# MLP input transposes as column-tiled unit-matrix products, one exponential quad more, and new order constants in a fused attention and MLP block

## Chip, core and metric

The kernel runs on one NeuronCore of a Trainium2 chip. Its metric is the device time of one execution in microseconds. Before the change it is 803.54 us, the median of three runs (803.52 to 803.60).

## What is computed

One transformer block with adaptive layer norm on 2048 tokens of width 640, with 32 heads of width 20, and an MLP of width 1536 without an activation (gate times up). Inputs and output are bf16.

```python
mod = (silu(c) @ w_mod).reshape(1, 6, 1, 640)      # sa, ca, ga, sb, cb, gb
h = layernorm(x) * (1 + ca) + sa
x = x + ga * attention(h, wqkv, wo)                # softmax(q k' / sqrt(20)) v, then wo
h = layernorm(x) * (1 + cb) + sb
x = x + gb * (((h @ w_gate) * (h @ w_up)) @ w_down)
```

## The kernel before

**Chunks, items, units.** The queries are cut into five chunks of 512, 512, 512, 256 and 256 tokens (`CHUNKS`). An item is one chunk with four of the 32 heads, so there are 40 items, 8 for each chunk: chunk 0 has items 0 to 7, chunk 4 items 32 to 39. The scores of an item are cut into units of 512 columns in one PSUM bank: 64 units for an item of a chunk of 512, 32 for one of 256. TensorE computes them (L1496) as row-tiled products with a contraction over 32 rows, one head in each of four row groups.

**Two ways to the exponential.** Most units go to ScalarE in groups of two: one instruction of 1024 columns each (L1534), 804 in all. The rest goes to VectorE in quads of four units. VectorE adds a constant and writes the score as a 16-bit integer (L1558, four times), makes two terms of it by masking (L1590 and L1598, 2048 columns each), and the first term is multiplied with the integer's own bits read as bf16, on VectorE (L1595, one instruction) or on GpSimd (L1650, four pieces). Both terms then take part in the product with V, so a quad costs twice the value products of the same units on ScalarE. `QUADS` holds the number of quads of each item, 110 in all.

**Products with V** (L2233) are column-tiled: four products with 32 output rows each run side by side and add into one PSUM bank. When an item is complete, VectorE and GpSimd normalise it (L1728 to L1742), and DMAs put it in place as input of the output projection.

**The suffix of a chunk.** When the eight items of a chunk are complete, `suffix(ci)` does the rest for its tokens: the output projection with residual, the second layer norm (`xn2`), its transposition into `h2T`, gate and up products, their product (`hprod`), and the down product with residual. Most of these products are column-tiled too and are built by `quarters` (L955). Those of the last chunk, the tail, are full-width products (L951). The suffix of a chunk runs between the scores of the next one. That of the last chunk has nothing beside it.

**The transposes.** In `suffix`, `h2_round` (L1968) makes one block of 128 features of `h2T` from up to four token tiles of `xn2`: each a full 128 x 128 TensorE transpose, with a bf16 result in PSUM that is read through `bankh(b)`. One instruction on VectorE, or on ScalarE in the tail, evacuates the block (L1975 and L1977) with scale and shift. Chunks 0 and 1 have 5 rounds of 4 transposes, chunk 2 has 10 rounds of 2 (its MLP begins in two halves of 256 tokens), chunks 3 and 4 have 5 rounds of 2.

**What sets the order.** The program's order is planned while it is built. A list scheduler (`Sched` and `pick_pe`) plays the five engines with a duration in ns for each task and writes down the order of instructions on each engine; on the chip, each engine then takes its instructions in just this order and waits on semaphores. A column-tiled product is planned as a list of four instructions in mode "P", a transpose as a single one in mode "X", scores in mode "S", and a change of mode counts about 100 ns. A transpose is planned at 57 ns (`C128`), the evacuation of n columns of `h2T` at n x .78 + 55 ns. `STAGE` overrides the planner's parameters for each item while that item's value products run: for example how late a quad's scores may be (`D_LATE`), how many value products are taken at once (`PVMIN`, `PVMAX`, `PVCAP`), how long PE is held for a score that is about to be ready (`HOLD`), and how late other work may make a score (`PVTOL`, `X_LATE`). Where PE would have too little to do, the planner inserts products of the unit matrix as filler (L2600).

Of the kernel before, what the change touches and what calls it, by code (L numbers as in the profile page):

```python
# [329 lines left out]
def emit_program(nc, sched, nsem_dma=56):  # L330
# [97 lines left out]
    with nc.Block() as block:  # L428
# [20 lines left out]
        def _(e):  # L449
# [23 lines left out]
EAGER = 7  # L473
# [75 lines left out]
    8: {"PVCAP": 15, "PVMAX": 5, "Z_LATE": 19.94, "FILL_Z": 3656.07, "FILL_MIN": 3946.65, "TPRIO": 0.57, "EAGER": 16, "PVMIN": 1, "XBACK": 0, "STEAL_GAP": 194.45, "XDPRIO": 2.05, "D_LATE": 22},  # L549
    9: {"X_LATE": -14.35, "PVCAP": 12, "XBACK": 0, "HOLD": 110, "PVMIN": 1, "D_LATE": 24, "D_RES": 23, "FILL_MIN": 4183.51, "XDPRIO": 1.15, "PVTOL": 224, "FILL_Z": 2258.51, "Z_LATE": -44.48},  # L550
    10: {"PVMAX": 9, "X_LATE": -167.91, "EAGER": 5, "D_LATE": 21, "PVCAP": 7, "XBACK": 0, "HOLD": 110, "FILL_Z": 3693.44, "Z_LATE": -95.95, "PVMIN": 1, "XDPRIO": 1.25, "PVTOL": 199, "D_RES": 17},
    11: {"DL": 0.443, "X_LATE": 54.31, "FILL_MIN": 4086.76, "PVTOL": 270, "PVMAX": 6, "PVCAP": 14, "D_LATE": 22, "Z_LATE": -74.79, "EAGER": 4},
    12: {"DL": 0.459, "D_LATE": 11, "STEAL_GAP": 248.0, "HOLD": 125, "FILL_Z": 3256.59, "PVMIN": 1, "D_RES": 29, "FILL_MIN": 4938.23, "PVMAX": 8},
    13: {"DL": 0.417, "D_RES": 4, "HOLD": 129, "PVMAX": 4, "TPRIO": 0.51, "PVMIN": 5, "STEAL_GAP": 145.61, "PVCAP": 13, "FILL_MIN": 5235.75, "FILL_Z": 2424.75, "PVTOL": 324, "Z_LATE": -67.84, "XDPRIO": 1.14},
    14: {"D_LATE": 14, "D_RES": 16, "FILL_MIN": 4279.59, "EAGER": 11, "X_LATE": -16.94, "PVTOL": 374, "FILL_Z": 3396.29, "HOLD": 95, "XDPRIO": 1.32, "PVMAX": 10, "TPRIO": 1.87, "PVCAP": 9, "XBACK": 1},
    15: {"X_LATE": -189.21, "EAGER": 15, "Z_LATE": -100, "D_RES": 5, "HOLD": 110, "PVMAX": 4, "PVMIN": 4, "PVTOL": 199, "STEAL_GAP": 191.33, "D_LATE": 14, "FILL_Z": 3394.6},
    16: {"D_RES": 64, "HOLD": 133, "PVCAP": 11, "PVMIN": 3, "PVTOL": 299, "EAGER": 7, "Z_LATE": 153.49, "FILL_Z": 2909.17, "D_LATE": 20, "X_LATE": 34.41, "PVMAX": 8, "XBACK": 1},
    17: {"D_LATE": 19, "PVMAX": 10, "PVMIN": 5, "FILL_MIN": 4052.05, "EAGER": 4, "PVCAP": 9, "XBACK": 4, "Z_LATE": 171.58, "TPRIO": 1.29, "HOLD": 80, "X_LATE": -94.24, "FILL_Z": 2893.25, "PVTOL": 199},
    18: {"FILL_MIN": 3727.81, "D_RES": 10, "X_LATE": 15.11, "FILL_Z": 2885.8, "HOLD": 80, "Z_LATE": -17.94, "PVTOL": 74, "XBACK": 1, "STEAL_GAP": 228.57, "EAGER": 7, "XDPRIO": 1.03, "TPRIO": 0.81},
    19: {"DL": 0.471, "D_LATE": 16, "FILL_MIN": 4973.79, "HOLD": 140, "TPRIO": 1.09, "PVCAP": 15, "X_LATE": 9.04, "PVMAX": 10, "FILL_Z": 3225.84, "STEAL_GAP": 168.9},  # L560
# [6 lines left out]
    26: {"DL": 0.411, "D_RES": 18, "X_LATE": -208.68, "PVMAX": 9, "PVCAP": 14, "STEAL_GAP": 200, "FILL_MIN": 4600.59, "PVMIN": 5, "EAGER": 10},
    27: {"DL": 0.473, "D_LATE": 6, "PVMAX": 10, "EAGER": 4, "D_RES": 72, "PVTOL": 249, "PVMIN": 1, "FILL_MIN": 4986.69, "HOLD": 80, "X_LATE": 41.47},
    28: {"PVCAP": 13, "X_LATE": 57.95, "D_RES": 23, "HOLD": 80, "FILL_Z": 3480.79, "XBACK": 3},
    29: {"PVCAP": 14, "PVMAX": 6, "D_RES": 46, "FILL_MIN": 3820.529, "PVTOL": 299, "X_LATE": 68.11, "Z_LATE": -100, "STEAL_GAP": 248.04, "FILL_Z": 3365.14, "EAGER": 11, "D_LATE": 12, "XBACK": 2},  # L570
# [12 lines left out]
STG_G0, STG_G, XC_G = 12, -10, -20
# [12 lines left out]
def build_kernel(nc, A_x, A_wqkv, A_wo, B_x, B_w_gate, B_w_up, B_w_down, c, w_mod, out):  # L596
# [1239 lines left out]
    def suffix(ci):  # L1836
# [128 lines left out]
        def h2_round(k, t_lo, t_hi):  # L1965
            mms = []
            for tl in range(t_lo, t_hi):
                f = lambda e, b, tl=tl, k=k: e.transpose(bankh(b)[:, tl * 128:(tl + 1) * 128],  # L1968
                                                         xn2[:, tl, k * 128:(k + 1) * 128], ident[:])
                mms.append((C128, f))  # L1970
            sl = slice(t_lo * 128, t_hi * 128)
            nn = (t_hi - t_lo) * 128

            def after(r, k=k):
                f = lambda e: e.tensor_scalar(h2T[:, k, sl], bankh(r.b["b"])[:, sl], mcol[:, 3, k:k + 1],  # L1975
                                              mcol[:, 2, k:k + 1], op0=ALU.mult, op1=ALU.add)
# [699 lines left out]
```

## Time and profile before

| | before |
|---|---|
| median of 3 runs | 803.54 us |
| profiled execution | 803.48 us |
| its span, first to last instruction | 801.7 us |
| granted TensorE clock | 1.000 |
| busy share: PE, VectorE, ScalarE, GpSimd | 98%, 88%, 95%, 44% |
| exponentials on ScalarE (L1534) | 804, from 15.9 us to 764.2 us (starts) |
| transposes for the MLP (L1968) | 80: 60 + 10 in chunks 0 to 3, 10 in the tail |
| their evacuations on VectorE (L1975) | 10 of 512 columns, 538 ns each; 17 of 256 columns |

Records of one engine overlap: the next instruction starts before the last one has written its result. The duration of a record is therefore longer than the step from one start to the next, and a busy share near 100% can hide small pauses. Where that matters, the text works with differences of start times. PE's matmul records are modelled at their ends.

### The profile page before, as it was taken

The page shows a single profiled execution, that of the slowest core. Times are in us where ns is not written, and L with a number is a line of the kernel's source. Part 1 is how long each engine was busy: PE and PEld are TensorE (multiplying, and loading weights), DVE is VectorE, ACT ScalarE, POOL GpSimd, SP SyncE. Part 2 cuts the span into 40 slices and gives each one's busy share as a digit, 9 for nine tenths or more (in the row PEclk, how much of TensorE's full clock was granted, in tenths as well). Part 3 has the DMA queues.
Part 4 walks back from the last instruction along what each step waited for, and adds up shares of the span by engine and source line. Part 5 has one row for each costly group of instructions (what it writes and reads, how often), then busy time and mean ns, then how long its engine had stood idle before and what let it go on. Part 6 is the DMA issues. An engine that isn't in the chain of part 4 may idle for free.

```text
span 801.7 us, 29815 instructions
## 1 busy us (share of the span) xinstructions
PE 787.4 (98%) x12817; PEld 306.7 (38%) x12817; DVE 704.7 (88%) x1301; ACT 760.3 (95%) x849; POOL 352.6 (44%) x359
## 2 busy tenths in 40 slices
PE   8999999999999999999999999999999999999998
PEld 4433333222233233233233322333344444445577
DVE  7979977999999899997998999998799897987863
ACT  7899999999999999999999999999999999999922
POOL 3303266564444452256546443443545554442610
DMA  9734211113320225100400121001203453003110
GB/s 311 212 87 108 69 46 34 51 35 116 99 69 26 51 68 171 27 6 24 104 6 22 44 64 37 7 23 47 64 5 70 97 130 73 13 23 95 41 38 17
DMA packets 108505, 52.72 MB, mean 66 GB/s; under 512 B 76051, under 2 KB 108375, under 8 KB 108375
## 3 DMA queue, kind: packets, MB, share of 16 engines
q1 hardware_dynamic: 107447, 49.67, 23.4%
q8 instruction: 102, 1.67, 0.9%
q10 hardware_dynamic: 928, 1.15, 0.4%
q14 instruction: 28, 0.23, 0.1%
HBM read 39.88 MB, written 8.41 MB: 60 GB/s over the span
## 4 chain that ended last, share of the span: by engine, by line
PE 50%; ACT 40%; issue 5%; DVE 3%; DMA 1%; ACTq 0%; DVEq 0%
ACT PP L1534 40%; PE ps_all L1496 16%; PE ps_all L955 14%; PE ps_all L2233 11%; PE ps_all L1215 3%; PE ps_all L951 3%; PE ps_all L1151 2%; DVE DB L1558 1%; DMA wm<-in_w_mod_dram 1%; PE ps_all L1112 1%; DVE DSS L1590 1%; PE ps_all L976 0%; DVE DSS L1598 0%; DVE DSS L1595 0%; PE ps_all L1968 0%
## 5 line engine op out<-in xcount | busy, mean ns | idle before, releaser
L1534 ACT ACTIVATE PP<-ps_all 128x1024 bf16<-128x1024 f32 x804 | 740.3, 1133 | 4.1 <-PE ps_all L1496 3.1
L1650 POOL TENSOR_TENSOR DSS<-DB,DSS 128x512 bf16<-128x512 bf16 x252 | 286.7, 1159 | 322.3 <-DVE DSS L1598 266.9
L1558 DVE TENSOR_SCALAR DB<-ps_all 128x512 int16<-128x512 f32 x440 | 293.4, 683 | 46.8 <-PE ps_all L1496 45.2
L1496 PE MATMUL ps_all<-QT,KT 32*128 32x512 bf16 (+1 forms) x2560 | 313.3, 340 | 7.3 <-ACT PP L1534 4.9
L1496 PEld LDWEIGHTS ps_all<-QT,KT 32*128 32x128 bf16 x2560 | 81.4, 91 | 257.9 <-ACT PP L1534 220.6
L2233 PE MATMUL ps_all<-PP,Vf 128*32 128x512 bf16 (+1 forms) x2016 | 158.0, 344 | 0.1
L955 PE MATMUL ps_all<-h2T,stg 128*32 128x512 bf16 (+2 forms) x1936 | 119.4, 327 | 1.0 <-DVE DB L1558 0.8
L2233 PE MATMUL ps_all<-DSS,Vf 128*32 128x512 bf16 (+2 forms) x1088 | 85.0, 341 | 0.0
L1590 DVE TENSOR_SCALAR DSS<-DB 128x2048 int16<-128x2048 int16 x110 | 76.1, 692 | 1.1 <-PE ps_all L2233 0.4
L1598 DVE TENSOR_SCALAR DSS<-DB 128x2048 int16<-128x2048 int16 x110 | 75.6, 687 | 0.0
L2233 PEld LDWEIGHTS ps_all<-PP,Vf 128*32 128x32 bf16 x2016 | 44.9, 94 | 78.9 <-issue 73.4
L955 PE MATMUL ps_all<-wd,hprod 128*32 128x320 bf16 (+1 forms) x1380 | 61.9, 279 | 0.0
L1595 DVE TENSOR_TENSOR DSS<-DB,DSS 128x2048 bf16<-128x2048 bf16 x47 | 59.8, 1272 | 0.1
L1734 POOL TENSOR_TENSOR OTn<-OT,invT 128x512 bf16<-128x512 f32 (+1 forms) x39 | 38.4, 984 | 40.8 <-DVE invT L1732 40.7
L955 PEld LDWEIGHTS ps_all<-h2T,stg 128*32 128x32 bf16 x1936 | 41.3, 95 | 36.0 <-issue 23.4
L955 PEld LDWEIGHTS ps_all<-wd,hprod 128*32 128x32 bf16 x1380 | 30.1, 96 | 21.1 <-issue 14.1
L2233 PEld LDWEIGHTS ps_all<-DSS,Vf 128*32 128x32 bf16 x1088 | 27.6, 95 | 18.3 <-issue 8.6
L955 PE MATMUL ps_all<-wV,hT 128*32 128x320 bf16 (+1 forms) x704 | 32.1, 289 | 0.0
L955 PE MATMUL ps_all<-wo,Ocp 128*32 128x320 bf16 (+1 forms) x648 | 30.0, 283 | 0.7 <-DVE xck L1929 0.3
L1215 PE MATMUL ps_all<-hT,wq 128*32 128x512 bf16 x375 | 30.7, 383 | 0.0
L1728 DVE STREAM_TRANSPOSE OT<-ps_all 128x512 f32<-128x512 f32 (+1 forms) x40 | 24.1, 602 | 2.7 <-PE ps_all L2233 2.6
L2091 DVE TENSOR_TENSOR hprod<-ps_all,gsb 128x512 bf16<-128x512 f32 x32 | 21.7, 679 | 4.3 <-PE ps_all L955 4.3
(134 smaller groups left out, 535.4 us busy)
## 6 DMA issues: line engine op xcount, KB each, us to landing
stg<-in_B_w_gate_dram SPq DMA_DIRECT2D x44, 160.0 KB
stg<-in_B_w_up_dram SPq DMA_DIRECT2D x44, 160.0 KB
QT<-q_rows SPq DMA_DIRECT2D x22, 128.0 KB
KT<-k_rows SPq DMA_DIRECT2D x84, 32.0 KB
wm<-in_w_mod_dram SPq DMA_DIRECT2D x3, 800.0 KB
x<-in_A_x_dram SPq DMA_DIRECT2D x7, 320.0 KB
wd<-in_B_w_down_dram SPq DMA_DIRECT2D x1, 1920.0 KB
out_dram<-xck SPq DMA_DIRECT2D x12, 160.0 KB
```

Of the source, the lines that this page charges most:

```text
L955: return lambda e, b: e.matmul(ps[32 * x:32 * x + 32, b, c0 + o:c0 + o + w], lhs()[:, 32 * x:32 * x + 32], rhs() if w == n else rhs()[:, o ...
L1215: f = [lambda e, b_, k=k, x=x: e.matmul(ps[x:x + min(32, w - x), b_, :], wx[:, k, r0 + x:r0 + min(x + 32, w)], hT[tc][:, k, :], tile_posit ...
L1496: ems.append(lambda e, i=i, kt=kt: e.matmul(dstf()[:, i * u.n:(i + 1) * u.n], KT[32 * u.s:32 * u.s + 32, u.j, kt * 128:(kt + 1) * 128], QT ...
L1534: return e.activation(PPs[g % 2][:, cellp["p"], 0:nu * 512], ps[:, b0:b0 + nu, :].rearrange("p b c -> p (b c)"), AFT.Exp, scale=ESCALE)
L1558: return e.tensor_scalar(DBl[st_["slot"]][:, x * 512:(x + 1) * 512], bank(cell["b"]), EBIAS, 0.0, op0=ALU.add, op1=ALU.max)
L1590: return e.tensor_scalar(DSl[st_["ss"][0]][:, :], DBl[st_["slot"]][:, :], 0x7F, 0x3F00, op0=ALU.bitwise_and, op1=ALU.bitwise_or)
L1595: return e.tensor_tensor(d, DBl[st_["slot"]][:, :].bitcast(BF16), d, ALU.mult)
L1598: return e.tensor_scalar(DSl[st_["ss"][1]][:, :], DBl[st_["slot"]][:, :], 0x7F80, 2, op0=ALU.bitwise_and, op1=ALU.bitwise_or)
L1650: return e.tensor_tensor(d, DBl[st_["slot"]][:, x * w:x * w + w].bitcast(BF16), d, ALU.mult)
L1728: t1 = Task("dve", n * 1.1 + 70, lambda e: e.transpose(OT[:, 0:n], ps[:, BPV, 0:n].rearrange("p (b q r) -> p b r q", q=32, r=2)), [], prio ...
L1734: f3 = lambda e: e.tensor_tensor(OTn[:, 0:n].rearrange("p (b c r) -> p b r c", c=32, r=2), OT[:, 0:n].rearrange("p (b r c) -> p b r c", c= ...
L2233: ems.append(lambda e, i=i, kt=kt, stt=stt, stp=stp: e.matmul(ps[32 * s:32 * s + mc, BPV, 0:u.n], Vf[:, (kt * H + 4 * u.j + s) * VW:(kt * ...
```

## The change

The change has three parts.

It makes the transposes of chunks 0 to 3 products with the unit matrix. `quarters(128, ...)` takes 32 columns of the `xn2` tile at a time as the stationary operand and the unit matrix as the moving one, in four column tiles, so that each transpose becomes four instructions in mode "P". The result is float in PSUM, and the evacuation reads it as float. The planner counts 65 ns (`H2Q_US`) instead of 57 for one. The evacuation's planned duration stays. The tail keeps its transposes.

It gives item 32, the first of chunk 4, two quads instead of one: 111 quads in all.

It replaces the rows of items 8 to 39 in `STAGE`. The rows of items 0 to 7 stay.

```diff
 QUADS = ...
-         (1, 2, 2, 1, 3, 0, 2, 2))
+         (2, 2, 2, 1, 3, 0, 2, 2))
 HALF = [0, 0, 4, 0, 0]
 RESID, RES_G = 1, -20
+H2Q, H2Q_US = 1, 65.0
 ...
 STAGE = {
 ...
-    13: {"DL": 0.417, "D_RES": 4, "HOLD": 129, "PVMAX": 4, "TPRIO": 0.51, "PVMIN": 5, "STEAL_GAP": 145.61, "PVCAP": 13, "FILL_MIN": 5235.75, "FILL_Z": 2424.75, "PVTOL": 324, "Z_LATE": -67.84, "XDPRIO": 1.14},
+    13: {"DL": 0.417, "D_RES": 4, "HOLD": 129, "PVMAX": 4, "TPRIO": 0.51, "PVMIN": 5, "STEAL_GAP": 145.61, "PVCAP": 13, "FILL_Z": 2424.75, "Z_LATE": -67.84, "XDPRIO": 1.14, "X_LATE": 6.51},
 ...
-    38: {"D_RES": 60, "PVMAX": 7, "PVTOL": 375, "D_LATE": 14, "EAGER": 5, "TPRIO": 0.3, "FILL_MIN": 3948.58, "XBACK": 3, "X_LATE": 4.46, "HOLD": 65},
+    38: {"D_RES": 63, "PVMAX": 4, "PVTOL": 375, "D_LATE": 14, "EAGER": 5, "TPRIO": 0.3, "FILL_MIN": 3948.58, "XBACK": 3, "HOLD": 65},
 ...
         def h2_round(k, t_lo, t_hi):
             mms = []
             for tl in range(t_lo, t_hi):
                 f = lambda e, b, tl=tl, k=k: e.transpose(bankh(b)[:, tl * 128:(tl + 1) * 128],
                                                          xn2[:, tl, k * 128:(k + 1) * 128], ident[:])
-                mms.append((C128, f))
+                if H2Q and not tail:
+                    f = quarters(128, lambda tl=tl, k=k: xn2[:, tl, k * 128:(k + 1) * 128], lambda: ident[:], True, True, tl * 128)
+                mms.append((H2Q_US if H2Q and not tail else C128, f))
             sl = slice(t_lo * 128, t_hi * 128)
             nn = (t_hi - t_lo) * 128
 
+            def h2b(b_):
+                return ps[:, b_, :] if H2Q and not tail else bankh(b_)
+
             def after(r, k=k):
-                f = lambda e: e.tensor_scalar(h2T[:, k, sl], bankh(r.b["b"])[:, sl], mcol[:, 3, k:k + 1],
+                f = lambda e: e.tensor_scalar(h2T[:, k, sl], h2b(r.b["b"])[:, sl], mcol[:, 3, k:k + 1],
                                               mcol[:, 2, k:k + 1], op0=ALU.mult, op1=ALU.add)
-                fa = lambda e: e.activation(h2T[:, k, sl], bankh(r.b["b"])[:, sl], AFT.Identity,
+                fa = lambda e: e.activation(h2T[:, k, sl], h2b(r.b["b"])[:, sl], AFT.Identity,
                                             bias=mcol[:, 2, k:k + 1], scale=mcol[:, 3, k:k + 1])
                 return [evac(nn, nn * .78 + 55, f, fa, [r.last, r_sb.evac[0], r_cb.evac[0]] + ...)]
```

More of the change, by code (lines that the diff above doesn't have):

```diff
@@ L567 @@
[L567 to L570, printed above, removed]
@@ new lines @@
+    10: {"PVMAX": 9, "X_LATE": -167.91, "EAGER": 5, "D_LATE": 21, "PVCAP": 11, "XBACK": 0, "HOLD": 110, "Z_LATE": -46.62, "PVMIN": 1, "XDPRIO": 1.25, "PVTOL": 199, "D_RES": 26, "FILL_Z": 3952.08, "TPRIO": 0.58, "FILL_MIN": 3141.24},
+    11: {"DL": 0.443, "X_LATE": -1.25, "FILL_MIN": 4196.55, "PVTOL": 270, "PVMAX": 6, "PVCAP": 14, "Z_LATE": -74.79, "EAGER": 1, "XBACK": 0, "FILL_Z": 2873.49},
+    12: {"DL": 0.459, "D_LATE": 11, "STEAL_GAP": 248.0, "HOLD": 125, "FILL_Z": 3256.59, "PVMIN": 1, "D_RES": 29, "FILL_MIN": 4598.1, "PVMAX": 9, "XDPRIO": 1.16, "XBACK": 3, "X_LATE": 38.58},
@@ new lines @@
+    16: {"D_RES": 55, "HOLD": 133, "PVCAP": 11, "PVMIN": 3, "PVTOL": 249, "Z_LATE": 153.49, "FILL_Z": 2909.17, "D_LATE": 20, "X_LATE": 34.41, "PVMAX": 8, "XBACK": 1, "STEAL_GAP": 218.51, "EAGER": 9},
+    17: {"D_LATE": 25, "PVMAX": 10, "PVMIN": 5, "FILL_MIN": 4191.37, "EAGER": 4, "PVCAP": 9, "XBACK": 4, "Z_LATE": 171.58, "TPRIO": 1.29, "HOLD": 80, "FILL_Z": 2893.25, "PVTOL": 224, "X_LATE": -5.25},
+    18: {"FILL_MIN": 3438.35, "D_RES": 10, "X_LATE": 15.11, "HOLD": 80, "Z_LATE": -17.94, "PVTOL": 124, "XBACK": 0, "STEAL_GAP": 228.57, "EAGER": 4, "XDPRIO": 1.03, "TPRIO": 0.81, "PVMIN": 1, "PVMAX": 10},
@@ new lines @@
+    19: {"DL": 0.471, "D_LATE": 16, "FILL_MIN": 4050.2, "HOLD": 140, "TPRIO": 1.09, "PVCAP": 15, "X_LATE": -24.6, "PVMAX": 10, "FILL_Z": 3225.84, "STEAL_GAP": 168.9, "EAGER": 5},
+    20: {"DL": 0.391, "D_LATE": 10, "PVCAP": 10, "FILL_Z": 4009.3, "HOLD": 65, "STEAL_GAP": 143.97, "X_LATE": 53.99, "PVTOL": 249, "EAGER": 5, "D_RES": 23, "PVMIN": 5},
+    21: {"D_RES": 10, "PVCAP": 20, "HOLD": 156, "PVMAX": 4, "PVMIN": 3, "FILL_MIN": 4085.58, "FILL_Z": 1888.49, "Z_LATE": 146.94, "EAGER": 9, "TPRIO": 0.3, "XDPRIO": 1.17, "PVTOL": 174, "X_LATE": 29.81, "STEAL_GAP": 187.71},
@@ new lines @@
+    22: {"PVMAX": 4, "FILL_MIN": 2795.19, "D_RES": 11, "EAGER": 6, "PVCAP": 8, "PVTOL": 224, "STEAL_GAP": 189.38, "FILL_Z": 4295.57, "HOLD": 215, "PVMIN": 5, "X_LATE": 162.88, "TPRIO": 0.77, "D_LATE": 10, "XBACK": 0},
+    23: {"PVTOL": 197, "PVMAX": 7, "D_RES": 26, "Z_LATE": -13.47, "STEAL_GAP": 116.18, "FILL_MIN": 4540.5, "EAGER": 11, "XDPRIO": 2.88, "TPRIO": 0.57, "XBACK": 0, "X_LATE": -12.6, "HOLD": 125},
+    24: {"DL": 0.464, "PVMAX": 11, "PVMIN": 4, "FILL_MIN": 3530.42, "EAGER": 7, "HOLD": 125, "XDPRIO": 0.3, "D_LATE": 14, "D_RES": 17, "PVTOL": 174, "Z_LATE": -64.18, "XBACK": 2, "X_LATE": 24.59, "FILL_Z": 2375.67},
@@ new lines @@
+    25: {"DL": 0.549, "STEAL_GAP": 200, "HOLD": 84, "X_LATE": -22.95, "D_RES": 19, "FILL_MIN": 3973.44, "PVCAP": 13, "D_LATE": 18, "PVMIN": 3, "Z_LATE": 116.92, "PVMAX": 6, "XBACK": 1, "EAGER": 9, "TPRIO": 0.68, "FILL_Z": 3555.45, "PVTOL": 274},
+    26: {"DL": 0.411, "D_RES": 12, "PVMAX": 9, "PVCAP": 14, "STEAL_GAP": 200, "FILL_MIN": 3869.09, "EAGER": 10, "XBACK": 2, "HOLD": 125, "X_LATE": -0.14},
+    27: {"DL": 0.473, "D_LATE": 6, "PVMAX": 8, "EAGER": 2, "D_RES": 80, "PVTOL": 249, "PVMIN": 1, "FILL_MIN": 5500, "HOLD": 80, "X_LATE": -6.15, "TPRIO": 0.3},
@@ new lines @@
+    28: {"PVCAP": 16, "D_RES": 23, "HOLD": 95, "FILL_Z": 2998.15, "XBACK": 0, "EAGER": 6},
+    29: {"PVCAP": 14, "PVMAX": 6, "D_RES": 46, "FILL_MIN": 3820.529, "PVTOL": 299, "X_LATE": 68.11, "Z_LATE": -100, "STEAL_GAP": 274.39, "FILL_Z": 3365.14, "D_LATE": 6, "XBACK": 2, "HOLD": 140, "EAGER": 8},
+    30: {"X_LATE": 126.74, "PVCAP": 19, "FILL_MIN": 3191.14, "D_LATE": 16, "EAGER": 6, "PVMAX": 7, "STEAL_GAP": 165.05, "PVTOL": 174, "XDPRIO": 2.13, "PVMIN": 1, "Z_LATE": -100, "HOLD": 110},
+    31: {"D_RES": 19, "FILL_MIN": 5203.54, "D_LATE": 13, "PVMIN": 1, "X_LATE": 13.6, "HOLD": 185, "PVTOL": 274, "PVCAP": 13, "EAGER": 10, "FILL_Z": 3497.58, "XDPRIO": 3.33, "STEAL_GAP": 99.46},
@@ new lines @@
+    35: {"PVMIN": 2, "PVMAX": 8, "FILL_MIN": 2704.26, "STEAL_GAP": 162.94, "X_LATE": -108.93, "HOLD": 61, "D_LATE": 8, "XBACK": 4, "XDPRIO": 0.37, "EAGER": 8, "TPRIO": 0.3, "D_RES": 20},
+    36: {"DL": 0.524, "PVMIN": 3, "D_RES": 10, "X_LATE": 8.69, "PVMAX": 8, "HOLD": 153, "PVCAP": 15, "STEAL_GAP": 333.93, "PVTOL": 149, "TPRIO": 0.92, "FILL_Z": 3611.42, "D_LATE": 18},
+    37: {"D_LATE": 12, "PVTOL": 104, "PVCAP": 13, "X_LATE": -65.91, "TPRIO": 0.3, "XDPRIO": 1.88, "HOLD": 35, "STEAL_GAP": 181.37, "PVMIN": 5, "FILL_MIN": 4037.77, "FILL_Z": 3731.25, "PVMAX": 6, "EAGER": 9, "D_RES": 26, "Z_LATE": 204.75},
@@ L581 @@
+    38: {"D_RES": 63, "PVMAX": 4, "PVTOL": 375, "D_LATE": 14, "EAGER": 5, "TPRIO": 0.3, "FILL_MIN": 3948.58, "XBACK": 3, "HOLD": 65},
+    39: {"D_LATE": 13, "PVTOL": 208, "X_LATE": -38.86, "PVCAP": 17, "PVMAX": 5, "EAGER": 8, "XBACK": 3, "TPRIO": 0.48, "HOLD": 0, "D_RES": 11},
 }
```

33 lines of the change are left out of this document (7 added, 26 removed).

## The prediction

> **What bounds the kernel now.** I read the page first (busy shares, groups), then the answer for the exponential's line, then the waits of two stretches, then the chain of its last 38 us. The exponential's line, L1534:
>
> ```profile
> L1534 ACT ACTIVATE PP<-ps_all x804: 1002/1130/1346, 15.9 to 764.2; 128x1024 bf16<-128x1024 f32 x161
>   PEld ps_all L1496: 220.6, 621
> ```
>
> 804 exponentials start between 15.9 and 764.2 us: 803 steps in 748.3 us. A record's 1130 ns overlaps the next one; read one by one, the starts lie 903 ns apart at the tenth percentile and at the median. 803 x 0.903 = 725.1 us, so ScalarE loses only 23.2 us to lateness: 11.7 in chunk 0 (206 groups), then 3.5, 2.7, 2.6 and 2.8 in chunks 1 to 4 (198, 196, 102, 102 groups). The span is 15.9 + 725.1 + 23.2 + 37.5 us after the last start = 801.7; the profiled execution took 803.48 (1.8 around the span), the median is 803.54, so differences carry over unchanged. The second line says that 621 times a score product (L1496) waited until an exponential freed its banks: ScalarE sets the pace. But not everywhere. Waits at 396-576 us, then at 670-764:
>
> ```profile
> PEld ps_all L1496 <- ACT PP L1534: 62.7, 187, 0.7
> ```
>
> ```profile
> PEld ps_all L1496 <- issue: 16.4, 74, 0.4
> PEld ps_all L1496 <- ACT PP L1534: 5.5, 19, 0.4
> ```
>
> In chunk 2 nearly each of 196 groups waits for ScalarE; in chunk 4 only 19 of 102 do, and 74 scores follow PE's earlier work directly. The chain behind the last exponential is PE without a break:
>
> ```profile
> 766.20 2.08 PE ps_all L955 x76
> 768.27 3.23 PE ps_all L951 x23
> ...
> 776.03 3.24 PE ps_all L955 x92
> 779.27 19.77 PE ps_all L951 x180
> ```
>
> PE's starts agree: from 620 us to the end I find no unexplained gap (over 0.42 ns a column, as 512 columns take 216, plus a change between kinds of products) except 0.56 us and 1.08 us of filler (L2600) between 720 and 740. So up to about 610 us ScalarE is the bound, after it PE, with ScalarE just behind.
>
> **The quad (item 32).** Four units leave ScalarE: two groups less, 2 x 0.903 = 1.81 us. On PE two score slots go: each 0.216 plus its two changes of product kind, 0.2 (512 columns to a score 323 ns instead of 216; score of 256 columns to the rest 202 instead of 109), 0.83 in all; the four scores ride in other score slots on free rows. The second term adds one round of value products, 0.216. PE gains 0.62. VectorE gets 4 x L1558, one L1590, one L1598 and the product on itself or on GpSimd:
>
> ```profile
> L1558 DVE TENSOR_SCALAR DB<-ps_all 128x512 int16<-128x512 f32 x440 | 293.4, 683 | 46.8 <-PE ps_all L1496 45.2
> L1650 POOL TENSOR_TENSOR DSS<-DB,DSS 128x512 bf16<-128x512 bf16 x252 | 286.7, 1159 | 322.3 <-DVE DSS L1598 266.9
> L1595 DVE TENSOR_TENSOR DSS<-DB,DSS 128x2048 bf16<-128x2048 bf16 x47 | 59.8, 1272 | 0.1
> ```
>
> Start to start these take 0.601, 0.60, 0.60, 1.13 (VectorE) or 4 x 1.117 (GpSimd): 3.6 to 4.7 us of VectorE. Item 32 and those behind it run here:
>
> ```profile
> 668.00:684.00 16.00, 16.00 (x318) 6.74 (x316) 11.42 (x21) 16.00 (x18) 7.28 (x8) 1.00 0.31 70
> 684.00:764.00 80.00, 79.86 (x1892) 41.27 (x1888) 67.30 (x132) 79.71 (x87) 36.22 (x38) 1.00 0.18 43
> ```
>
> VectorE (third pair) has 17.3 us idle of 96: it hides the quad; uncovered, up to 4.7 us would come back as late banks. The worth lies between 0.62 (PE the bound) and 1.81 (ScalarE). Chunk 4 is nearer to PE: 0.62 + 19/102 x 1.19 = 0.84. If no row were free, the two slots would stay and nothing be gained.
>
> **The transposes.** 70 of them (5 blocks x 4, 4, 4, 2 tiles; the last chunk keeps its 10) become 280 column-tiled products. Before, around chunk 0's:
>
> ```profile
> 258.81 0.34 PE L1968 MATMUL ps_all<-ident,xn 128*128 128x128 bf16 x3
> 259.08 0.39 PE L1496 MATMUL ps_all<-QT,KT 32*128 32x512 bf16 x3
> ...
> 261.21 0.40 PE L1968 MATMUL ps_all<-ident,xn 128*128 128x128 bf16 x4
> 261.54 0.40 PE L2600 MATMUL ps_all<-ident 128*32 128x512 bf16 x4
> ```
>
> Transposes follow each other after 56 ns; the first column-tiled product behind one after 149, so leaving costs 93, and entering from a 512-column value product takes 333 instead of about 222, some 110. The same 128 columns as four column tiles (halved L955 products) also follow at 56: the product itself is free. Entries from column-tiled work number 7 before 764 us, exits to it 8: 7 x 0.11 + 8 x 0.093 = 1.5 us of PE at most. The 14 exits that lead to scores (163 ns) gain nothing: tiled work pays the same (166). What lateness there is to win: the 28 exponentials beside these transposes lost 0.99 us, at the average rate of chunks 1 to 4 (19 ns) it would be 0.53. I take 0.46, between 0 and 1.5. The Trainium skill (TensorEngine Tiling (Array Packing), Tiling Modes, Key Properties) says that changing the tiling mode drains TensorE; the 149 against 56 ns agrees.
>
> **Their evacuations.** L1975 now reads float:
>
> ```profile
> L1975 DVE TENSOR_SCALAR h2T<-ps_all,mcol 128x512 bf16<-128x512 bf16 x10 | 5.1, 538 | 1.0 <-PE ps_all L1968 0.9
> L1227 DVE TENSOR_SCALAR KPA<-ps_all 128x512 bf16<-128x512 f32 x13 | 8.8, 679 | 0.7 <-PE ps_all L1215 0.7
> ```
>
> Start to start 452 against 601 ns at 512 columns, 319 against 331 at 256: 10 x 0.149 + 15 x 0.012 = 1.7 us of VectorE. The order's cost stays nn x .78 + 55 = 454 ns, so VectorE falls behind by up to 0.75 us in each of chunks 0 and 1. Next transposes wait for its banks, scores queue behind them on PE, ScalarE behind those. An example: at 734 us, where the order counts 255 ns and the chip takes 319, one exponential came 0.32 us late. One such stall in each of two chunks is 0.6; between 0 and 1.7 I take 0.3, since VectorE has idle time in both (5.1 of 60 us at 240-300).
>
> **The order of items 8 to 39.** The trace can't show it; its rows bound it. Items 8, 13, 26 and 37 lose 0.70, 1.03, 0.59 and 0.92 us where the median item loses about 0.27: 2.2 us that single late waits made (the largest, 0.6 us at 342, is PE waiting for L1558). All items at the median would be 2.8 us less than now; all of chunks 1 and 2 at chunk 4's rate (27.6 ns a group instead of 15.6) 4.7 us more. DMA issues on SP move with the order; the engines are 18% busy at 684-764, so I count them at nothing; a late weight block would hold one PE round. I take -0.9, under half of the four items' excess and the filler at 734.
>
> Sum: -0.84 - 0.46 + 0.3 - 0.9 = -1.9: 803.5 - 1.9 = **801.6**.
>
> **Rivals.** (1) Given back: quad at PE's 0.62, transposes 0.46, evacuations at 1.3, order no better: +0.2, or +0.8 with the transposes at nothing; with evacuations at 0.5, -0.6: 803.0 to 804.2. For it: 74 direct follow-ups in chunk 4. Chance 0.22. (2) The transposes don't do what they say, since the order sets them between scores (14 exits already are): quad 0.84, evacuations 0.3: 803.0. Chance 0.12. (3) Slower: the new order reaches scores late. In chunks 1 and 2, PE's room per group is small; at chunk 4's rate +4.7 - 0.84 - 0.46 + 0.3 = 807.2. It decides from 2.6 us more lateness, 6.7 ns per group over 394 groups (22.3 instead of 15.6). Against it: 187 of 196 groups there wait for ScalarE, so most lateness is absorbed. Chance 0.10. (4) The four quarters run in series, 3 x 56 ns more for each of 70: 11.8 us of PE, of which chunk 3's 1.7 are uncovered: 803.3 to 813.4 with the rest as forecast, say 808. Against it: groups of four start within 30 ns of each other. Chance 0.02. The Trainium skill (Perfetto Trace Analysis, Optimizing Tensor Performance, Transposes) speaks against the change here: a logical transpose should use the transpose, not a standard matmul. The equal 56 ns don't bear that out.
>
> **How the numbers follow.** About 0.2% (1.6 us) is what a measurement of this kernel can tell from no change. Forecast 0.54, faster; rivals 1 and 2 0.34, within; 3 and 4 0.12, slower. Low end: transposes at 1.5 and the order at -2.2: -0.84 - 1.5 + 0.3 - 2.2 = -4.2, 799.3; I give 799.4. The high end goes past rival 1 to 804.8 and leaves rivals 3 and 4 out.
>
> **What would show it.** 802 exponentials; no L1968 in 128*128 form before 764 us; L1975 at about 680 ns with float input; the first 213 us (items 0 to 7) unchanged; the last exponential start 1 to 3 us earlier. If that start is 2 us earlier while the stretch behind it grows over 37.5 us by about 1, PE is the bound as read. Chunk 1 and 2 lateness over 22 ns per group would make the forecast wrong; over 0.5 us beside chunk 0's evacuations makes their term too small.

## The result, and the profile after

The changed kernel takes **805.57 us**, the median of ten executions (805.0 to 806.51). The kernel before took 803.51 beside it (ten, 803.46 to 803.62). The ratio is 1.0027, with a 95% interval of 1.0018 to 1.0036: slower by about 2 us, where 1.9 us less had been forecast. The profiled execution took 806.49 us with a span of 804.7. It lies 0.9 above the median: TensorE's granted clock was at half for 3.4 us in it. That need not be the whole reason, since two of the ten, with a mean clock of 1.000, took 806.32 and 806.38.

The answer for the exponential's line after the change comes first (minimum, median and maximum ns, then first and last start; below it the idle time of ScalarE by what ended it, and who waited for ScalarE):

```profile
L1535 ACT ACTIVATE PP<-ps_all x802: 1003/1127/1346, 15.9 to 767.3; 128x1024 bf16<-128x1024 f32 x161
  PE ps_all L1497: 6.6, 12
  PEld ps_all L1497: 222.3, 613
```

There are 802 exponentials, two fewer, as forecast, yet the last one starts 3.1 us later (767.33 against 764.22). Read from the start times as before, with 0.903 us for each step, lateness (what the exponentials start later in all than at that even pace) is 28.1 us instead of 23.2. By chunks:

| lateness, us | all | chunk 0 | 1 | 2 | 3 | 4 | beside the MLP transposes |
|---|---|---|---|---|---|---|---|
| before | 23.2 | 11.72 | 3.48 | 2.67 | 2.56 | 2.79 | 1.05 |
| after | 28.1 | 11.73 | 5.57 | 4.09 | 3.61 | 3.12 | 4.91 |

The last column adds up five stretches, one for each set of rounds of `h2_round` and its evacuations (from the first transpose to 2 us behind the last evacuation): 0, 0.25, 0.18, 0.28 and 0.34 us before; 1.29, 1.18, 0.91, 0.31 and 1.21 after. So the bill of the two profiled executions is: -1.81 for the two exponentials, +3.86 beside the transposes, +1.05 elsewhere in items 8 to 39, -0.09 behind the last exponential; together +3.0, and 806.49 - 803.48 is 3.01. The first 213 us are unchanged. Some 1.4 us of the "elsewhere" are the stretch at half clock, read at the end of this document.

What happened beside the transposes is seen in the groups of after (busy us, mean ns of one, idle before):

```profile
L1981 DVE TENSOR_SCALAR h2T<-ps_all,mcol 128x512 bf16<-128x512 f32 x10 | 7.6, 803 | 0.7 <-PE ps_all L956 0.6
L956 PE MATMUL ps_all<-ident,xn 128*32 128x128 bf16 x240 | 7.2, 222 | 0.4 <-DVE h2T L1981 0.2
L1981 DVE TENSOR_SCALAR h2T<-ps_all,mcol 128x256 bf16<-128x256 f32 x10 | 4.8, 527 | 0.0
```

The 240 products are the 60 transposes of chunks 0 to 2, four each, and the fours start some 56 ns apart, as forecast. The evacuation of 512 columns has a mean of 803 ns, not about 680 as the prediction's marker had it, and 538 before. Start to start it takes 719 ns for 512 columns and 452 for 256, against 452 to 456 and 319 before, and against 454 and 255 in the plan. The longest of the waits that end with these evacuations (us in all, times, longest), after and then before; `h2Tt` is chunk 3's block:

```profile
PEld ps_all L956 <- DVE h2T L1981: 2.6, 7, 0.9
PE ps_all L1497 <- DVE h2T L1981: 1.5, 4, 0.6
PEld ps_all L956 <- DVE h2Tt L1981: 1.5, 3, 0.9
```

```profile
PEld ps_all L1968 <- DVE h2T L1975: 0.7, 3, 0.3
PEld ps_all L955 <- DVE h2T L1975: 0.6, 2, 0.3
```

With the smaller rows, TensorE's products and weight loads, which overlap, have 8.0 us of such waits where they had 2.4: TensorE waits for what VectorE has yet to evacuate, and five times the waiting product is a score (four of them above). One such place on the timeline of after, in chunk 1 (start, duration, engine, and in brackets the idle time before):

```profile
433.65 0.57 PE L956 MATMUL ps_all<-ident,xn 128*32 128x128 bf16 x28
433.94 2.97 DVE L1981 TENSOR_SCALAR h2T<-ps_all,mcol 128x512 bf16<-128x512 f32 x4 [0.62 <-PE ps_all L956]
...
435.62 0.39 PE L1497 MATMUL ps_all<-QT,KT 32*128 32x512 bf16 x3 [0.19 <-DVE h2T L1981]
...
436.97 0.40 PE L956 MATMUL ps_all<-h2T,stg 128*32 128x512 bf16 x4 [0.62 <-DVE h2T L1981]
...
437.30 0.39 PE L1497 MATMUL ps_all<-QT,KT 32*128 32x512 bf16 x3
...
437.73 1.02 ACT L1535 ACTIVATE PP<-ps_all 128x1024 bf16<-128x1024 f32 x1 [0.66 <-PE ps_all L1497]
```

Four evacuations run back to back on VectorE. TensorE reaches the gate and up products (436.97), which read `h2T`, and stands idle for 0.62 us. The score planned behind them (437.30) comes late, and the exponential that wants it starts after ScalarE has been idle for 0.66 us.

The other views shown before. TensorE's waits at 670 to 764 us:

```profile
PEld ps_all L1497 <- issue: 14.0, 64, 0.4
...
PEld ps_all L1497 <- ACT PP L1535: 7.8, 30, 0.4
```

and the chain behind the last exponential:

```profile
769.22 2.07 PE ps_all L956 x76
...
782.29 19.77 PE ps_all L952 x180
```

Before, 19 scores waited for ScalarE here and 74 followed TensorE's earlier work; now 30 and 64. The pieces of the chain have the same lengths (those between are 3.23 and 3.24 us for 23 and 92 products, as before), and the stretch behind the last exponential is 37.4 us as before (37.5).

### The profile page after: what moved, and what is told of

It is laid out like the page before. It is cut to its first block, busy times and chain, and to the rows that moved or that the text cites. A ratio compares the mean times of both kernels' runs of the same rounds, so it can differ in the third digit from the quotient of the medians.

```text
span 804.7 us, 30172 instructions
## 1 busy us (share of the span) xinstructions
PE 787.9 (98%) x12987; PEld 306.6 (38%) x12987; DVE 712.2 (89%) x1307; ACT 759.7 (94%) x847; POOL 356.5 (44%) x363
## 4 chain that ended last, share of the span: by engine, by line
PE 63%; ACT 29%; DVE 4%; issue 3%; POOL 0%; ACTq 0%; DVEq 0%; POOLq 0%
ACT PP L1535 29%; PE ps_all L1497 20%; PE ps_all L956 18%; PE ps_all L2239 14%; PE ps_all L1216 3%; PE ps_all L952 3%; PE ps_all L1152 2%; DVE h2T L1981 1%; PE ps_all L2604 1%; DVE DB L1559 1%; PE ps_all L1113 1%; PE ps_all L2606 0%; PE ps_all L977 0%; DVE DSS L1599 0%; DVE DSS L1591 0%
## 5 line engine op out<-in xcount | busy, mean ns | idle before, releaser
L1651 POOL TENSOR_TENSOR DSS<-DB,DSS 128x512 bf16<-128x512 bf16 x256 | 291.2, 1157 | 332.2 <-DVE DSS L1599 276.2
L956 PE MATMUL ps_all<-h2T,stg 128*32 128x256 bf16 (+2 forms) x1980 | 120.5, 325 | 0.9 <-DVE h2T L1981 0.6
L2239 PE MATMUL ps_all<-DSS,Vf 128*32 128x512 bf16 (+2 forms) x1104 | 87.1, 341 | 0.4 <-DVE DSS L1599 0.3
L1591 DVE TENSOR_SCALAR DSS<-DB 128x2048 int16<-128x2048 int16 x111 | 77.7, 700 | 2.0 <-PE ps_all L2239 1.4
L1599 DVE TENSOR_SCALAR DSS<-DB 128x2048 int16<-128x2048 int16 x111 | 77.5, 698 | 0.0
L1596 DVE TENSOR_TENSOR DSS<-DB,DSS 128x2048 bf16<-128x2048 bf16 x47 | 57.3, 1223 | 0.1
L956 PEld LDWEIGHTS ps_all<-h2T,stg 128*32 128x32 bf16 x1980 | 43.4, 96 | 35.6 <-issue 22.8
L1735 POOL TENSOR_TENSOR OTn<-OT,invT 128x512 bf16<-128x512 f32 (+1 forms) x39 | 36.6, 939 | 36.5 <-DVE invT L1733 36.2
```

The source lines that it names most:

```text
L956: return lambda e, b: e.matmul(ps[32 * x:32 * x + 32, b, c0 + o:c0 + o + w], lhs()[:, 32 * x:32 * x + 32], rhs() if w == n else rhs()[:, o ...
L1591: return e.tensor_scalar(DSl[st_["ss"][0]][:, :], DBl[st_["slot"]][:, :], 0x7F, 0x3F00, op0=ALU.bitwise_and, op1=ALU.bitwise_or)
L1596: return e.tensor_tensor(d, DBl[st_["slot"]][:, :].bitcast(BF16), d, ALU.mult)
L1599: return e.tensor_scalar(DSl[st_["ss"][1]][:, :], DBl[st_["slot"]][:, :], 0x7F80, 2, op0=ALU.bitwise_and, op1=ALU.bitwise_or)
L1651: return e.tensor_tensor(d, DBl[st_["slot"]][:, x * w:x * w + w].bitcast(BF16), d, ALU.mult)
L1735: f3 = lambda e: e.tensor_tensor(OTn[:, 0:n].rearrange("p (b c r) -> p b r c", c=32, r=2), OT[:, 0:n].rearrange("p (b r c) -> p b r c", c= ...
```

## The experiments

Each row of `STAGE` for items 8 to 39 is called an order constant here. "Planned" is what the list scheduler counts for a task, "run" is what the chip takes. Every median stands beside the kernel before on the same chip (803.49 to 803.53). The experiments that take the transposes back to bf16 come first.

**The new order with true transposes in the column tiles.** The plan and the order are those of after; only the operation and its result in PSUM differ.

```diff
-f = quarters(128, lambda tl=tl, k=k: xn2[:, tl, k * 128:(k + 1) * 128], lambda: ident[:], True, True, tl * 128)
+f = [lambda e, b, tl=tl, k=k, x=x: e.transpose(bankh(b)[32 * x:32 * x + 32, tl * 128:(tl + 1) * 128],
+         xn2[:, tl, k * 128 + 32 * x:k * 128 + 32 * x + 32], ident[:], tile_position=(0, 32 * x)) for x in range(4)]
...
-return ps[:, b_, :] if H2Q and not tail else bankh(b_)
+return bankh(b_)
```

> The changed kernel, with the 280 products replaced by 280 transposes in the same four column tiles, so that PSUM again holds bf16. Durations planned and order of instructions are those of the changed kernel. Theory A (VectorE's evacuation of float with column scalars steps 719 and 452 ns where the order counts 454 and 255, so VectorE falls behind, PE waits for its banks and ScalarE for PE): evacuations back to about 452 and 319 ns, lateness beside the transposes from 4.9 back to about 1.1 us, no half-clock stretch, time about 801.7. Theory B (four instructions per transpose cost PE): 805 as in the changed kernel. Theory C (the new order constants are the loss): 805.

Measured: 802.05 us (801.34 to 804.51, 11 executions), ratio 0.9985 [0.9976, 0.9994]. The evacuations take some 452 and 319 ns again, lateness falls from 28.1 to 23.2 (1.4 of it is the stretch at half clock, which this profile lacks), and beside the transposes from 4.91 to 1.27. The group of the evacuations:

```profile
L1983 DVE TENSOR_SCALAR h2T<-ps_all,mcol 128x512 bf16<-128x512 bf16 x10 | 5.0, 537 | 1.3 <-PE ps_all L1972 1.3
```

The order of instructions is that of after to the last one, so 3.5 us of the change's time hang on what the product leaves, float instead of bf16.

**The new constants and the quad without the products.** `H2Q` is 0, all else as after, planned anew.

```diff
-H2Q, H2Q_US = 1, 65.0
+H2Q, H2Q_US = 0, 65.0
```

> The changed kernel with full-width transposes as before; the 111th quad and the new constants stay. A and B: lateness beside the transposes about 1.1 us, the quad's 1.8 us kept, about 801.8. C: 805 or more.

Measured: 811.81 us (4 executions), 1.0103 [1.009, 1.0117]. One wait of ScalarE for value products, in item 26 at 604 to 613 us, makes 3.4 us of it; the rest is spread over many shorter ones (the next, at 698 us, is 1.6) and 1.45 us behind the last exponential. That one wait left out, lateness beside the transposes is 1.05, as before. The number would fit theory C, but the version with full transposes in the order of after, further below, speaks against it. This run doesn't say what the constants are worth, since the plan around them changed: a transpose planned as one task of 57 ns in its own mode gives another order than four column-tiled products of 65 ns in mode "P".

**The products alone, with the old constants and the old quads.**

```diff
-         (2, 2, 2, 1, 3, 0, 2, 2))
+         (1, 2, 2, 1, 3, 0, 2, 2))
...
-STAGE rows 8 to 39 of after
+STAGE rows 8 to 39 of before
```

> The kernel before with the column-tiled products alone: 110 quads and the old constants. A and B: lateness beside the transposes 4 to 5 us instead of 1.1, about 807. C: 803.5.

Measured: 816.83 us (815.27 to 819.12, 5 executions), 1.0172 [1.0158, 1.0186]: neither forecast came. ScalarE's waits at 604 to 622 us:

```profile
ACT PP L1535 <- PE ps_all L2239: 9.7, 1, 9.7
```

and what TensorE does meanwhile, from this run's timeline:

```profile
609.60 0.39 PE L1497 MATMUL ps_all<-QT,KT 32*128 32x256 bf16 x4
609.92 1.49 PE L956 MATMUL ps_all<-h2T,stg 128*32 128x256 bf16 x48
...
614.98 0.29 PE L956 MATMUL ps_all<-ident,xn 128*32 128x128 bf16 x8 [1.21 <-DVE h2T L1981]
...
616.66 0.95 PE L956 MATMUL ps_all<-h2T,stg 128*32 128x256 bf16 x28 [1.06 <-DVE h2T L1981]
...
618.42 0.84 PE L2239 MATMUL ps_all<-PP,Vf 128*32 128x256 bf16 x24
```

The order runs the suffix of chunk 2 for 8.5 us without a score in between; the value products that free ScalarE's output buffers come behind it. Waits for VectorE's evacuations are some 2.3 us of that, the rest is how it was planned. Here too the plan changed together with what was to be measured.

**The true duration of the evacuations in the plan.** All as after, the evacuation planned at 719 and 452 ns.

```diff
-return [evac(nn, nn * .78 + 55, f, fa, ...
+return [evac(nn, nn * 1.043 + 185 if H2Q and not tail else nn * .78 + 55, f, fa, ...
```

> The changed kernel with the evacuation planned at 719 ns for 512 columns and 452 for 256 (n x 1.043 + 185) instead of 454 and 255. A, if the wrong plan is what hurts: the planner puts other work around the longer evacuations, lateness beside the transposes 1 to 2.5 us, 802 to 803.5. A, if the longer evacuation itself hurts however it is planned: 804.5 to 805.5. B and C: 805.

Measured: 819.14 us (4 executions), 1.0194 [1.018, 1.0208]: a miss. Again ScalarE waits in item 26, once: the exponential behind the one at 610.8 us comes 10.3 us late. A plan that knows the truth is no better with constants that were chosen for a plan that doesn't.

These three cost 8 to 16 us, of which single waits make 3.4, 9.8 and 10.3, in orders that the change of a planned figure or of the constants had upset. The next four therefore leave the order of before or of after untouched and change only what an instruction does: the function that a planned task issues is replaced, its planned mode and duration stay.

**The new order with full transposes.** Where after issues four products, one full-width transpose with a bf16 result stands; planned as in after.

```diff
-f = quarters(128, lambda tl=tl, k=k: xn2[:, tl, k * 128:(k + 1) * 128], lambda: ident[:], True, True, tl * 128)
+f = [lambda e, b, tl=tl, k=k: e.transpose(bankh(b)[:, tl * 128:(tl + 1) * 128], xn2[:, tl, k * 128:(k + 1) * 128], ident[:])]
...
-return ps[:, b_, :] if H2Q and not tail else bankh(b_)
+return bankh(b_)
```

> The changed kernel's order of instructions with one full-width transpose in place of each four products (bf16 in PSUM again); 111 quads and the new constants. Theory A (the float evacuations are the loss, the form of the product on PE matters little): lateness beside the transposes about 1.2 to 1.8 us instead of 4.9; against e4_tiled_transpose only the two changes of tiling, about 0.1 us each where the order put a transpose beside column-tiled work, so 802 to 803. If changes of tiling cost as much as the forecast allowed (1.5 us): 803.5. If the half-clock stretches come from column-tiled unit products: none here; if from the order: some of the runs at 0.998 again.

Measured: 801.92 us (801.61 to 802.6, 11 executions), 0.998 [0.9971, 0.9989]. The exponential's line:

```profile
L1535 ACT ACTIVATE PP<-ps_all x802: 1002/1136/1345, 16.3 to 763.2; 128x1024 bf16<-128x1024 f32 x161
  PE ps_all L1497: 3.1, 5
```

ScalarE waits for scores 5 times (3.1 us) where after has 12 (6.6 us). The order and the quad without the products are thus 1.6 us faster than before, and the products take 3.65 us from that. This version is faster than both kernels; it and the one with tiled transposes differ by 0.13 us, which these executions don't tell apart.

Its start times say where the 1.6 us are: two exponentials fewer save 1.81, lateness is 23.6 instead of 23.2, and the stretch behind the last exponential is 0.1 shorter. The order itself won no lateness.

**The old order with the products.** The reverse: before, each transpose's task issues the four products, and the evacuation reads float.

```diff
+if not tail:
+    def f(e, b, tl=tl, k=k):
+        q = quarters(128, lambda: xn2[:, tl, k * 128:(k + 1) * 128], lambda: ident[:], True, True, tl * 128)
+        return [g(e, b) for g in q][-1]
...
-f = lambda e: e.tensor_scalar(h2T[:, k, sl], bankh(r.b["b"])[:, sl], ...
+f = lambda e: e.tensor_scalar(h2T[:, k, sl], (bankh(r.b["b"]) if tail else ps[:, r.b["b"], :])[:, sl], ...
```

> The order of instructions of the kernel before, kept exactly, with four products in place of each transpose and float evacuations. Theory A: lateness beside the transposes 4 to 5 us instead of 1.05, evacuations stepping 719 and 452 ns, 806.5 to 807.5, without the single 10 us wait of e2_products_only, which is the order's. If that wait came with the products themselves: 815 or more. Theory C (the new constants are the loss): 803.5.

Measured: 806.82 us (806.56 to 807.53, 5 executions), 1.0042 [1.003, 1.0055]. The group of its evacuations and the two largest sums of waits for them:

```profile
L1979 DVE TENSOR_SCALAR h2T<-ps_all,mcol 128x512 bf16<-128x512 f32 x10 | 7.5, 802 | 0.5 <-PE ps_all L955 0.5
```

```profile
PEld ps_all L955 <- DVE h2T L1979: 3.2, 7, 0.8
PE ps_all L955 <- DVE h2T L1979: 1.5, 4, 0.5
```

The products cost 3.3 us in the old order too, with the same 802 ns; lateness beside the transposes is about 4 us instead of 1.05.

**The old order with tiled transposes.** As the last, with the four column-tiled transposes and a bf16 result.

```diff
+if not tail:
+    def f(e, b, tl=tl, k=k):
+        return [e.transpose(bankh(b)[32 * x:32 * x + 32, tl * 128:(tl + 1) * 128],
+                            xn2[:, tl, k * 128 + 32 * x:k * 128 + 32 * x + 32], ident[:],
+                            tile_position=(0, 32 * x)) for x in range(4)][-1]
```

> The order of instructions of the kernel before, kept exactly, with four column-tiled transposes (bf16) in place of each full-width one. It measures the changes of tiling alone: 803.0 to 803.5 if ScalarE hides them, 802.0 if all of PE's 1.5 us counts. If four instructions cost PE (theory B): 804 or more.

Measured: 803.43 us (803.3 to 804.45, 11 executions), 1.0001 [0.9992, 1.001]. Column tiles in place of full transposes, with nothing else, make no difference that shows, though TensorE is rid of the changes of tiling: the step to column-tiled work behind a transpose is 56 ns instead of 149, and the one from a 512-column value product into a transpose 216 to 226 instead of 324 to 333. Lateness is 23.1 against 23.2: the saved changes are worth next to nothing on the time.

**After, with constants for scale and shift.** The evacuations still read float, but multiply by 1.0 and add 0.0 in place of the columns of `mcol` (chunks 0 to 3 then lack the second layer norm's modulation).

```diff
-f = lambda e: e.tensor_scalar(h2T[:, k, sl], h2b(r.b["b"])[:, sl], mcol[:, 3, k:k + 1], mcol[:, 2, k:k + 1], ...
+f = lambda e: e.tensor_scalar(h2T[:, k, sl], h2b(r.b["b"])[:, sl], mcol[:, 3, k:k + 1] if tail else 1.0,
+                              mcol[:, 2, k:k + 1] if tail else 0.0, ...
```

> The changed kernel with the float evacuation's scale and shift columns replaced by the constants 1 and 0 (it leaves out the second layer norm's scale and shift in chunks 0 to 3). If the two column scalars are what makes 719 ns of the forecast's 601: steps of about 601 and 331 ns, lateness beside the transposes 2 to 3 us, 803 to 804. If reading float is the whole price: 719 and 452 as in the changed kernel, 805.5.

Measured: 802.67 us (802.36 to 803.75, 11 executions), 0.9991 [0.9983, 1.0].

```profile
L1981 DVE TENSOR_SCALAR h2T<-ps_all 128x512 bf16<-128x512 f32 x10 | 6.4, 682 | 1.0 <-PE ps_all L956 1.0
```

Now the instruction reads no column, like the row that the prediction priced it by (L1227, which multiplies by one constant and takes 679 ns): 682 ns, and start to start 598 and 331. So the forecast's price was right for constants and wrong for columns.

**bf16 with constants, and float with one column.** The version with tiled transposes and the constants; and after with the scale's column kept and the shift a constant (chunks 0 to 3 then lack the modulation in the first, its shift in the second).

```diff
-f = lambda e: e.tensor_scalar(h2T[:, k, sl], h2b(r.b["b"])[:, sl], mcol[:, 3, k:k + 1], mcol[:, 2, k:k + 1], ...
+f = lambda e: e.tensor_scalar(h2T[:, k, sl], h2b(r.b["b"])[:, sl], mcol[:, 3, k:k + 1],
+                              mcol[:, 2, k:k + 1] if tail else 0.0, ...
```

> e4_tiled_transpose with the constants 1 and 0 instead of the scale and shift columns (it leaves out the second layer norm's scale and shift in chunks 0 to 3). The fourth cell beside bf16 with columns (452 and 319 ns), float with constants (598 and 331) and float with columns (719 and 452). If two columns cost about 120 ns whatever is read: about 330 and 200. If they cost only where float is read: 452 and 319.

> The changed kernel with the scale column kept and the shift replaced by the constant 0 (it leaves out the second layer norm's shift in chunks 0 to 3). If each column costs the same: about 660 and 390 ns a step. If one column is enough for the whole price: 719 and 452. If only the second costs: 598 and 331.

Measured, one execution each, which can't tell a few tenths apart: 802.03 and 804.08 us.

```profile
L1983 DVE TENSOR_SCALAR h2T<-ps_all 128x512 bf16<-128x512 bf16 x10 | 3.9, 419 | 1.7 <-PE ps_all L1972 1.7
```

```profile
L1981 DVE TENSOR_SCALAR h2T<-ps_all,mcol 128x512 bf16<-128x512 f32 x10 | 7.0, 745 | 0.8 <-PE ps_all L956 0.8
```

With these the price of an evacuation is known but for bf16 with one column (start to start, ns), and with it the time of five versions in one order. "VectorE more" is 10 evacuations of 512 columns and 15 of 256, each against 452 and 319:

| evacuation | 512 columns | 256 columns | VectorE more, us | time, us |
|---|---|---|---|---|
| bf16, two constants | 342 | 198 | -2.9 | 802.03 (one execution) |
| bf16, two columns | 452 to 456 | 319 | 0 | 802.05 |
| float, two constants | 598 | 331 | 1.6 | 802.67 |
| float, one column | 658 | 392 | 3.2 | 804.08 (one execution) |
| float, two columns (after) | 719 | 452 | 4.7 | 805.57 |

Evacuations shorter than before's win nothing that the one execution shows. Of longer ones, 0.4 (0.62 of 1.6) to 0.75 (3.52 of 4.7) of VectorE's extra time comes back as time of the kernel; the 0.62 is near what these executions can tell apart.

**The quad alone.** Before with the one entry of `QUADS`, planned anew with the old constants.

```diff
-         (1, 2, 2, 1, 3, 0, 2, 2))
+         (2, 2, 2, 1, 3, 0, 2, 2))
```

> The kernel before with the 111th quad alone: full-width transposes, old constants. If the quad's worth stands by itself: 801.7 (803.5 less 1.8), with the lateness of items 8 to 39 at 11.5 us as before. If the constants fit only the plan they were searched for (as in e1_no_products and e2_products_only): a long wait somewhere behind the first decision that the quad changes, 804 to 815, and items far ahead of chunk 4 as before.

Measured: 805.63 us (805.6 to 806.29, 9 executions), 1.0027 [1.0017, 1.0037]. Again a single wait, now in item 37 (725 to 740 us), for value products:

```profile
ACT PP L1534 <- PE ps_all L2233: 2.2, 1, 2.2
```

Lateness is 2.1 us above before's, which cancels the 1.81 of the two exponentials, and the stretch behind the last exponential is 39.25 us instead of 37.46. Against this, the new constants in the plan made for them (801.92, with the same quad and full transposes) are worth 3.7 us.

## Why the prediction was wrong

**The evacuations' term is the step that failed.** It counted 1.7 us of VectorE, took 0.3 of them as time, and had 1.7 as its far end. The runs show 4.7 us of VectorE and 3.3 (old order) to 3.65 us (new order) of time. Two things were wrong in it. The price came from rows that read no column for a scale or shift: L1227, a float evacuation with one constant, at 512 columns, and at 256 columns the 331 ns that float copies such as L1809 take. This instruction takes scale and shift from `mcol`, one column of SBUF each, and each adds about 60 ns: 598, 658, 719. Before's own rows held the right price. L1975's 319 ns at 256 columns include what the two columns of `mcol` cost. For each column of PSUM that is read, L1975 takes 0.52 to 0.535 ns ((452 to 456, less 319)/256), and float rows take about 1.055 ((601 - 331)/256). The difference gives an estimate of 452 to 456 ns at 256 columns and 722 to 726 at 512; 452 and 719 are what was measured. The Trainium skill (VectorE: DVE Perf Modes, Why PSUM operands drop a tier) has the same: an operand in PSUM allows at most the twofold rate, and only the single rate for fp32. The trace agrees, with 1.04 against about 0.53 ns a column, and an estimate by that rule, twice the time of each column, would have given about 4.7 us. Then, "VectorE has idle time" was no cover. Idle time of an engine over 60 us doesn't help a wait of 1 us: TensorE takes its products in the planned order, so an evacuation that is 0.6 us late holds the score behind it, and ScalarE with it, as the timeline at 437 us shows. Even at the forecast's own price the term was some 0.62 to 0.75 us (802.67 against 802.05 and 801.92), not 0.3. The marker "over 0.5 us beside chunk 0's evacuations" was met, with 1.29.

**The transposes' term (-0.46) was nothing that shows:** 803.43 against 803.49 in the old order, 802.05 against 801.92 in the new one. That TensorE's changes of tiling are real (some 93 to 110 ns) and that the exits to scores gain nothing was as read; the others lay in its slack, so the outcome is that of rival 2 for this term. The products themselves cost TensorE no more than transposes do, so rival 4 didn't occur.

**The quad and the order** together were forecast at -1.74 and measured at -1.57 (801.92 against 803.49). That they agree is luck. The prediction gave the quad 0.84 of ScalarE's 1.81 and the order 0.9 less lateness; the start times of 801.92's profile show all of the 1.81 and 0.4 more lateness. With the old constants the quad costs 2.1 us, so what it is worth hangs on the order. The order's bounds (-3.5 to +4.7) came from rows of before, and these don't bound it: three re-planned orders cost 8 to 16 us, 3.4 to 10.3 of it through one long wait each. Why the planner puts so much of chunk 2's suffix ahead of item 26's value products when a planned figure changes was not tried.

**"After 610 us TensorE is the bound"** didn't show its marker in the new order: the last exponential of the full-transpose version starts at 763.2, 1.0 us earlier, and the stretch behind it is 37.36 us, as before. That fits ScalarE's price for the quad, 1.81, better than 0.84, though the new constants changed chunk 4 too. In the quad-only run that stretch grew by 1.8 us, which is half of the marker; the other half, an earlier last exponential, is missing (764.75). So the -0.84 isn't settled as a term of its own.

**The rivals.** Rival 1, "given back", named the mechanism that decided, with evacuations at 1.3; at 3.65 it crosses to slower. (Its +0.8 is +0.7: 1.3 - 0.62.) Rival 3's sign came true, and in the profile its marker too: 9.66 us of lateness in chunks 1 and 2 are 24.5 ns per group. Without the 1.4 us of the stretch at half clock, which lies in chunk 1, they are about 21, under the 22 that it had named. Its cause didn't come true: without the float evacuations the same order has 3.1 to 3.3 us in chunk 1, instead of 5.57.

## What to carry to other kernels

Price a changed instruction by its rate and its fixed part separately, from rows that agree with it in each: here the type in PSUM set the rate and the column operands set the fixed part, and one row that had the first but not the second gave a third of the cost. In an order that is fixed beforehand, an instruction that takes longer can cost time where others wait for its result (here 0.4 to 0.75 of what it takes longer), however idle its engine is on average; making it shorter than before won nothing here. To measure an edit in a planned kernel, keep the planned figures and replace only what the task issues, or the plan's own response hides the effect.

## What the hardware showed

A scale or shift read from a column of SBUF costs VectorE's tensor-scalar instruction about 60 ns each over a constant, at 256 and 512 columns, bf16 and float alike (start to start: 198 to 319 and 342 to about 452 for two with bf16, 598 to 658 to 719 for one and two with float).

A full 128 x 128 transpose and four column-tiled transposes or unit products of 32 columns each take TensorE the same time where one follows another: 56 ns in before, in the two versions with tiled transposes and in after. In the old order, the kernel's time is 803.43 with four tiled transposes and 803.49 with the full one. The Trainium skill (Perfetto Trace Analysis, Optimizing Tensor Performance, Transposes) prefers the transpose, and the times agree with its advice: 801.92 and 802.05 with transposes, 805.57 with products. In this case what counts is the bf16 result in PSUM that a transpose can leave.

In the profiled execution of after the granted clock was 0.5 for 3.41 us, at 262.8 to 266.2, just behind chunk 0's late evacuations; between 227 us and the drop TensorE's longest idle time is 0.41 us. The windows of 260 to 280 us, before and after (busy us of TensorE, weight loads, VectorE, ScalarE, GpSimd, then the granted clock, the DMA share and GB/s):

```profile
260.00:280.00 20.00, 19.95 (x262) 6.22 (x264) 17.59 (x31) 20.00 (x23) 8.29 (x9) 1.00 0.21 52
```

```profile
260.00:280.00 20.00, 19.01 (x264) 5.74 (x264) 16.77 (x27) 18.07 (x20) 7.22 (x7) 0.91 0.20 49
```

It cost some 1.4 us there: two exponentials came 1.05 and 0.39 us late (265.4 and 266.7). A mean clock of 0.998 appeared in 2 of 10 executions of after, in 2 of 11 of the new order with tiled transposes, and in 2 of 5 of the products with old constants, where one more had 0.996; in no execution of the other versions, among them 11 each of the new order with full transposes, of the old order with tiled transposes and of after with constants for scale and shift. So few executions don't tie it to the tiling, the order or the product, and its cause stays open.
